# Putting transposed 16-bit planes back together on ScalarE and GpSimd, in place of ScalarE alone

## The chip, the cores and the metric

The kernel runs on one core of a Trainium2 chip. The metric is the device time of one execution in microseconds (us), taken as the median of several runs. The engines are named as in the profile: PE is TensorE, with PEld for its weight loads; DVE is VectorE, ACT is ScalarE, POOL is GpSimd, and SP is the engine that issues nearly all DMAs here (SPq is its queue). Every engine works through its own list of instructions strictly in the order in which that list was written, and waits where a datum or a buffer is not there yet.

## The reference: what is computed

Top-k attention for 4 batches of 8 heads (576 positions, head size 64), whose output is the input of a mixture of 8 experts with Sinkhorn-balanced gates:

```python
scores = q @ k.T / sqrt(64)                     # per batch and head, 576 x 576
kth    = 32nd largest of each row
attn   = softmax(where(scores >= kth, scores, -1e9))
x      = (attn @ v) as 2304 rows of 512
P      = exp(x @ w_gate - max); 8 rounds of normalising rows and columns
out    = sum over 8 experts e of P[:, e] * (relu(x @ w1[e]) @ w2[e])
```

## The kernel before

All of it is one program whose instructions are put in order ahead of time: each part has a priority, and a planner with estimated durations writes one list for each engine. Attention has priority over the expert matmuls, which fill TensorE between its pieces. So while attention runs, TensorE alternates between scores (L122, L123), weighing the values (L281) and expert matmuls (L488, L601).

**Attention.** For two heads at a time and tiles of 128 queries, TensorE makes scores in `sp`, a PSUM tile of which there is one; ScalarE copies them to `s` (L134); VectorE finds the 32 largest in four rounds of MAX8 and MATCH_REPLACE8 (L144, L147); GpSimd makes a bias `eb` (L148); ScalarE runs two passes over the row (L150, L151); GpSimd and VectorE make the reciprocal sum (L199, L200), and GpSimd scales the weights (L203). The weights `Et` (queries on partitions) must then be turned, so that keys are on partitions, into the tile `at` (one buffer), which the matmuls of L281 read.

**The turning.** For the first two stages TensorE turns them. Once more than four pieces of `x` exist, a DMA does, and it turns 16-bit elements. `cross` therefore splits the 32-bit weights on ScalarE into two planes of 16-bit halves (`halves`, L164), has SP issue the transposing DMA into `turned` (L168), and appends to the list `turning` a function `whole` that interleaves the two turned planes into `at` (L171). `land` runs what is in that list. It is called with `tc.issue_after(...)`, which puts the instructions of the block that are on the same engine behind a given one: behind the second pass of a later softmax (`topk`) or behind the next split (`cross`). `halves` and `turned` have one buffer each. A smaller variant, `cross_rest` (L181 to L194), does the same for the 64 left-over queries, and is left as it is.

**Experts.** Weights are loaded into `wr` (3 buffers, L470), rounded to `wh` on ScalarE (L83) and the rest `wl` computed on GpSimd (L86); `wh` and `wl` have 6 buffers each. ScalarE writes the hidden layer `hh` (L556) and VectorE its rest `hl` (L557); ScalarE moves outputs out of PSUM (`y`, L609). After attention, from about 1030 us on, only expert work is left.

Of the kernel before, what the change touches and what calls it, by code (L numbers as in the profile page):

```python
# [9 lines left out]
U16 = mybir.dt.uint16  # L10
AF = mybir.ActivationFunctionType
# [40 lines left out]
def kernel(  # L52
# [11 lines left out]
    nc = tc.nc  # L64
# [93 lines left out]
    def land():  # L158
        while turning:
            turning.pop(0)()  # L160

    def cross(Et, at):
        halves = ap_.tile([128, 2, 2 * S], U16, name="halves", bufs=1)
        split = nc.scalar.activation(halves, Et.bitcast(U16).rearrange("p a (b h) -> p h (a b)", h=2), AF.Copy)  # L164
        with tc.issue_after(split.ins):
            land()
        turned = ap_.tile([128, 2, 9, 128], U16, name="turned", bufs=1)
        nc.sync.dma_start_transpose(turned.rearrange("p h g c -> p (h g) c"), halves.rearrange("p h k -> p (h k)"))  # L168

        def whole():  # L170
            nc.scalar.activation(at.bitcast(U16).rearrange("p g (c h) -> p g c h", h=2),  # L171
                                 turned.rearrange("p h g c -> p g c h"), AF.Copy)

        turning.append(whole)

# [705 lines left out]
```

## Time and profile before

| | |
|---|---|
| median of 3 runs | 1831.21 us (1831.04 to 1831.55) |
| the profiled execution's own time | 1833.39 us |
| its span, first to last instruction | 1831.6 us |
| mean granted TensorE clock | 0.996 of full speed |
| instructions | 26304 |

The rows further down come from the profiled execution. The profiler's span is 1.8 us shorter than that execution's own time, which itself is 2.2 us above the median. A matmul's end in the profile is modelled, so that matmuls overlap on paper: with 512 columns each is shown at about 0.39 us, while the next one starts 0.23 us later. Engine idle times therefore are best read where the next start is late.

### The profile page before, as it was taken

What the parts mean: (1) busy time and instruction counts of PE and PEld (TensorE: products, weight loads), DVE (VectorE), ACT (ScalarE), POOL (GpSimd) and SP (SyncE); (2) the same over time, 40 slices, a digit from 0 to 9 for tenths busy, and PEclk for the clock granted to TensorE, in tenths of its full rate; (3) what the DMA queues carried; (4) which work ended last, traced back from release to release, by engine and by line L of the source; (5) the groups of instructions that cost most, each with busy time, mean ns of one, the idle gap of its engine ahead of it and who ended that gap; (6) DMA issues with size and microseconds to landing.
All of it is one profiled execution on the core that took longest, in us unless ns stands there. A gap on an engine that the chain in (4) does not pass through costs nothing.

```text
span 1831.6 us, 26304 instructions
## 1 busy us (share of the span) xinstructions
PE 1785.6 (97%) x9385; PEld 1480.7 (81%) x9385; DVE 1207.9 (66%) x2232; ACT 1187.6 (65%) x1785; POOL 1068.3 (58%) x842
## 2 busy tenths in 40 slices
PE   4989999999999999999999999999999999999998
PEld 3777888888888878777787889888888888888887
DVE  8999998988888878878787141255555555533333
ACT  5888899999999888988897645533333333333331
POOL 4367856656766585556564688955544554554441
PEclk9999999999999999999999999999999999999999
DMA  4885877765767575656655356423333333211111
GB/s 136 264 260 174 255 198 178 207 191 160 199 174 179 143 223 170 168 152 164 172 152 142 90 174 217 161 98 109 114 117 104 104 107 114 90 58 63 53 35 46
DMA packets 227203, 270.77 MB, mean 148 GB/s; under 512 B 142464, under 2 KB 146688, under 8 KB 227072
## 3 DMA queue, kind: packets, MB, share of 16 engines
q1 hardware_dynamic: 226928, 268.83, 49.8%
q8 instruction: 73, 1.20, 0.3%
q14 instruction: 58, 0.48, 0.1%
q10 hardware_dynamic: 144, 0.26, 0.0%
HBM read 202.19 MB, written 34.60 MB: 129 GB/s over the span
## 4 chain that ended last, share of the span: by engine, by line
PE 83%; ACT 4%; POOL 4%; DVE 3%; DMA 3%; issue 3%; SPq 0%; ACTq 0%; POOLq 0%
PE p L601 20%; PE p L775 19%; PE p L488 18%; PE p L713 10%; PE pc L713 5%; PE pt L281 4%; DMA wr<-in_w_dram 2%; PE pb L713 2%; POOL wl L86 2%; PE sp L122 2%; PE sp L123 2%; DVE m L144 1%; DVE w L147 1%; PE p L524 1%; ACT wh L83 1%
## 5 line engine op out<-in xcount | busy, mean ns | idle before, releaser
L86 POOL TENSOR_TENSOR wl<-wr,wh 128x1024 fp32r<-128x1024 f32 x288 | 694.0, 2422 | 456.2 <-ACT wh L83 445.7
L83 ACT ACTIVATE wh<-wr 128x1024 fp32r<-128x1024 f32 x288 | 304.1, 1061 | 284.4 <-PE p L713 191.2
L144 DVE MAX8 m<-w 128x8 f32<-128x576 f32 x432 | 320.6, 753 | 5.8
L488 PE MATMUL p<-xh,wh 128*128 128x256 f32 (+1 forms) x832 | 274.7, 330 | 2.8 <-DVE hl L557 1.9
L488 PE MATMUL p<-xl,wh 128*128 128x256 f32 (+1 forms) x832 | 273.7, 329 | 0.1
L488 PE MATMUL p<-xh,wl 128*128 128x256 f32 (+1 forms) x832 | 273.0, 328 | 0.0
L601 PE MATMUL p<-wh,hh 128*128 128x512 f32 x640 | 250.2, 396 | 4.3 <-ACT hh L556 2.8
L601 PE MATMUL p<-wl,hh 128*128 128x512 f32 x640 | 249.6, 392 | 0.0
L601 PE MATMUL p<-wh,hl 128*128 128x512 f32 x640 | 241.3, 392 | 0.0
L147 DVE MATCH_REPLACE8 w<-m,w 128x576 f32<-128x576 f32 x288 | 213.7, 743 | 0.0
L775 PE MATMUL p<-wh,h2h 128*128 128x512 f32 x512 | 199.1, 389 | 0.6 <-DVE acc L618 0.6
L775 PE MATMUL p<-wl,h2h 128*128 128x512 f32 x512 | 199.2, 389 | 0.0
L775 PE MATMUL p<-wh,h2l 128*128 128x512 f32 x512 | 196.3, 389 | 0.0
L618 DVE SCALAR_TENSOR_TENSOR acc<-p,P,acc 128x512 f32<-128x512 f32 x120 | 89.5, 750 | 160.4 <-PE p L775 160.4
L557 DVE SCALAR_TENSOR_TENSOR hl<-p,hh 128x512 fp32r<-128x512 f32 x160 | 109.0, 682 | 106.5 <-ACT hh L556 105.5
L488 PEld LDWEIGHTS p<-xh,wh 128*128 128x128 f32 x832 | 157.6, 189 | 20.8 <-issue 2.1
L488 PEld LDWEIGHTS p<-xl,wh 128*128 128x128 f32 x832 | 157.7, 189 | 15.7 <-issue 0.9
L488 PEld LDWEIGHTS p<-xh,wl 128*128 128x128 f32 x832 | 157.6, 189 | 14.2 <-issue 0.5
L144 DVE MAX8 m<-s 128x8 f32<-128x576 f32 x144 | 108.4, 753 | 85.3 <-ACT s L134 84.8
L601 PEld LDWEIGHTS p<-wh,hh 128*128 128x128 f32 x640 | 120.1, 188 | 31.7 <-ACT hh L556 5.3
L601 PEld LDWEIGHTS p<-wl,hh 128*128 128x128 f32 x640 | 120.6, 188 | 23.4 <-issue 0.4
L601 PEld LDWEIGHTS p<-wh,hl 128*128 128x128 f32 x640 | 119.9, 188 | 23.6 <-DVE hl L557 0.2
(171 smaller groups left out, 3550.4 us busy)
## 6 DMA issues: line engine op xcount, KB each, us to landing
wr<-in_w_dram SPq DMA_DIRECT2D x248, 512.0 KB, 3.5
y<-y SPq DMA_DIRECT2D x160, 256.0 KB, 2.8
raw<-in_k_dram SPq DMA_DIRECT2D x48, 288.0 KB, 3.7
p<-y SPq DMA_DIRECT2D x32, 256.0 KB, 4.0
wr<-in_w_dram SPq DMA_DIRECT2D x32, 256.0 KB, 4.3
yp<-p SPq DMA_DIRECT2D x32, 256.0 KB, 3.3
raw<-in_q_dram SPq DMA_DIRECT2D x31, 256.0 KB, 3.5
values<-in_v_dram SPq DMA_DIRECT2D x24, 256.0 KB, 3.6
```

Of the source, the lines that this page charges most:

```text
L83: nc.scalar.activation(dst, src, AF.Copy)
L86: nc.gpsimd.tensor_tensor(dst, src, hi.bitcast(F32), op=OP.subtract)
L122: nc.tensor.matmul(o, qc, kh[:, cs], start=(i == 0), stop=False)
L144: nc.vector.max(m8[:, u, r, :], ws[u] if r else units[u][0])
L147: nc.vector.match_replace(ws[u], m8[:, u, r, :], ws[u] if r else units[u][0], LOWEST)
L281: weighed = nc.tensor.matmul(av[r, 0:n], vr[:, o:o + 64], at[:, block, 0:n], start=(j == order[0]), stop=(j == order[-1]))
L488: nc.tensor.matmul(ps[:, fo, :], a[:, kk, fs], x[:, k0 + kk, cs], start=(i == 0), stop=(i == 3 * nk - 1))
L557: nc.vector.scalar_tensor_tensor(seat.hl[:, ft, cs], src, 0.0, seat.hh[:, ft, cs].bitcast(F32), op0=OP.max, op1=OP.subtract)
L601: nc.tensor.matmul(ps, a[:, ft, ts], m[:, ft % 2, :], start=(i == 0), stop=(i == 3 * NFT - 1))
L618: return nc.vector.scalar_tensor_tensor(ACC[t], y, g, ACC[t], op0=OP.mult, op1=OP.add)
L713: nc.tensor.matmul(ps, w[:, kk, :], x[:, kk, :], start=(fresh and i == 0), stop=(i == 5), skip_group_check=True)
L775: nc.tensor.matmul(ps, a[:, ft, ts], m[:, ft, :], start=(i == 0), stop=(i == 11))
```

## The change

The one ScalarE instruction of `whole`, which writes all 2304 16-bit elements of each partition, becomes two: ScalarE writes the elements with index 0 of each pair, and GpSimd those with index 1. Each half reads one plane in order and writes every other 16-bit element of `at`. The smaller variant in `cross_rest` stays on ScalarE.

```diff
         def whole():
-            nc.scalar.activation(at.bitcast(U16).rearrange("p g (c h) -> p g c h", h=2),
-                                 turned.rearrange("p h g c -> p g c h"), AF.Copy)
+            au = at.bitcast(U16).rearrange("p g (c h) -> p g c h", h=2)
+            two = turned.rearrange("p h g c -> p g c h")
+            nc.scalar.activation(au[:, :, :, 0], two[:, :, :, 0], AF.Copy)
+            nc.gpsimd.tensor_copy(au[:, :, :, 1], two[:, :, :, 1])
 
         turning.append(whole)
```

## Rows read from the trace of the kernel before

**Rows 1.** The page, parts 1 and 2: busy time; tenths in 40 slices.
```profile
PE 1785.6 (97%) x9385; PEld 1480.7 (81%) x9385; DVE 1207.9 (66%) x2232; ACT 1187.6 (65%) x1785; POOL 1068.3 (58%) x842
...
PE   4989999999999999999999999999999999999998
```

**Rows 2.** Windows: length, busy us (count) of PE, PEld, DVE, ACT, POOL; clock; DMA.
```profile
220.00:1030.00 810.00, 804.19 (x4612) 664.92 (x4610) 658.60 (x1291) 728.69 (x1056) 488.36 (x428) 1.00 0.64 174
...
1110.00:1800.00 690.00, 689.53 (x3160) 575.98 (x3159) 309.66 (x428) 248.44 (x352) 372.97 (x243) 1.00 0.31 99
```

**Rows 3.** Waits of PE, 220 to 1030 us: us in total, times, longest.
```profile
PE sp L122 <- ACT s L134: 1.8, 2, 1.4
PE p L601 <- ACT hh L556: 1.6, 1, 1.6
PE p L601 <- ACT y L609: 1.4, 1, 1.4
PE p L488 <- DVE hl L557: 0.8, 2, 0.6
```

**Rows 4.** Tile `turned`: duration ns min/median/max; waiters (us, times); landings.
```profile
L168 SPq DMA_TRANSPOSE turned<-halves x48: 2405/2740/4628, 222.6 to 1009.8; - x48
L171 ACT ACTIVATE at<-turned x48: 2381/2404/2447, 233.0 to 1016.6; 128x2304 uint16<-128x2304 uint16 x48
...
  PEld pt L281: 0.4, 1
...
DMA to landing us min/median/max: 3.3/4.6/7.1
```

**Rows 5.** Groups by form, ACT, 220 to 1030 us: busy us, mean ns.
```profile
L164 ACT ACTIVATE halves<-Et 128x2304 uint16<-128x2304 uint16 x48 | 101.9, 2124 | 15.3 <-POOL Et L203 13.9 <-DMA turned<-halves 1.1
...
L181 ACT ACTIVATE halves<-Et 128x1152 uint16<-128x1152 uint16 x12 | 14.0, 1169 | 6.1 <-DMA turned<-halves 3.8 <-POOL Et L203 2.2
```

**Rows 6.** Groups by form, POOL, 220 to 1030 us.
```profile
L86 POOL TENSOR_TENSOR wl<-wr,wh 128x1024 fp32r<-128x1024 f32 x128 | 306.9, 2410 | 120.9 <-ACT wh L83 112.5 <-PE p L488 4.6 <-issue 2.5
L203 POOL TENSOR_SCALAR Et<-Et,st 128x576 f32<-128x576 f32 x107 | 79.0, 750 | 25.6 <-DVE st L200 23.8 <-PE sp L123 0.7 <-PE p L488 0.3
...
L86 POOL TENSOR_TENSOR qm<-raw,qm 64x256 fp32r<-64x256 f32 x15 | 11.1, 738 | 1.2 <-POOL eb L148 0.2
...
L199 POOL TENSOR_SCALAR st<-st 128x2 f32<-128x2 f32 x47 | 9.0, 191 | 51.4 <-ACT Et L151 49.4
```

**Rows 7.** Timeline of PE around three gaps: start us, us, [idle before].
```profile
419.58 0.50 PE L601 MATMUL p<-wh,hh 128*128 128x512 f32 x1 [1.62 <-ACT hh L556]
...
817.16 0.50 PE L601 MATMUL p<-wh,hh 128*128 128x512 f32 x1 [1.41 <-ACT y L609]
...
842.04 0.40 PE L122 MATMUL sp<-kh,qs 128*128 128x288 f32 x1 [1.38 <-ACT s L134]
```

**Rows 8.** Timeline of ACT, the same three places.
```profile
416.66 2.39 ACT L171 ACTIVATE at<-turned 128x2304 uint16<-128x2304 uint16 x1
418.95 0.57 ACT L556 ACTIVATE hh<-p 128x512 fp32r<-128x512 f32 x1
...
811.51 2.40 ACT L171 ACTIVATE at<-turned 128x2304 uint16<-128x2304 uint16 x1
813.82 0.63 ACT L134 ACTIVATE s<-sp 128x576 f32<-128x576 f32 x1
814.35 0.77 ACT L150 ACTIVATE Et<-s,m 128x576 f32<-128x576 f32 x1
...
839.08 2.39 ACT L171 ACTIVATE at<-turned 128x2304 uint16<-128x2304 uint16 x1
841.37 0.62 ACT L134 ACTIVATE s<-sp 128x576 f32<-128x576 f32 x1
```

**Rows 9.** Timeline of DVE, second place: start us, us.
```profile
812.79 0.76 DVE L144 MAX8 m<-w 128x8 f32<-128x576 f32 x1
```

**Rows 10.** Waits of PEld, and of SP's queue, 220 to 1030 us.
```profile
PEld p L601 <- POOL wl L86: 0.3, 1, 0.3
...
SPq L470 <- POOL wl L86: 163.3, 67, 5.5
```

## The prediction

> **What bounds the kernel now.** I read the busy times first, because they say which engine can set the end at all. TensorE is busy for 97% of the span and every other engine for 66% or less, and after the first slices its row of tenths shows nothing but nines [rows 1]. So the time is the sum of TensorE's work, which this change leaves alone, and of the gaps in it. A change on two other engines can only move gaps.
>
> Next, the windows, to see which gaps lie where the change acts. All 48 instructions that it replaces start between 233.0 and 1016.6 us [rows 4]. In the stretch from 220 to 1030 us TensorE is busy for 804.19 of 810 us, at full clock: 5.8 us of gaps. In the expert stretch after it, from 1110 to 1800 us, the gaps are 0.5 us [rows 2]. The start of the kernel has many more, but lies ahead of the first changed instruction. This gives the size of the question: if every gap of the stretch vanished, the kernel would gain 5.8 us, 0.3%. The loss has no such cap.
>
> Then the waits of TensorE in that stretch. They sum to 5.6 us, and 4.8 of them name ScalarE: the score copy 1.8, the hidden layer 1.6, the output copy 1.4; the other 0.8 names VectorE [rows 3]. GpSimd is not among them, and weight loads waited for its `wl` for 0.3 us once [rows 10]. In the same stretch ScalarE is busy for 728.69 us (90%) and GpSimd for 488.36 (60%) [rows 2]. The engine that loses work is the one that TensorE waits for; the one that gets it is not.
>
> Last, the timeline at the three large gaps, to see what held ScalarE there. Each has a whole copy L171 ahead of the late instruction. At 416.66 the copy runs 2.39 us, the hidden layer `hh` starts behind it at 418.95, and TensorE, after a gap of 1.62, goes on at 419.58. At 839.08 it runs 2.39 us, the score copy follows at 841.37, and TensorE goes on at 842.04 after 1.38. At 811.51 it runs 2.40 us, and behind it stand a score copy at 813.82, the softmax passes from 814.35 on and the output copy for which TensorE waited 1.41 us until 817.16 [rows 7, 8]. These three are 4.4 of the 5.8 us.
>
> **The ScalarE half.** Removed: 48 instructions of 2.404 us on 2304 elements [rows 4]. Added: 48 on 1152 elements, reading in order and writing every other 16-bit element. The nearest row has the same count and a stride on the other side: L181, 1.169 us [rows 5]. Below, the bound is half of L164, 2.124 / 2 = 1.062, which pretends that the fixed cost halves as well; above it is half of L171 plus a fixed cost taken from L164 and L181, 2 x 1.169 - 2.124 = 0.214, half of which is missing when an instruction is cut in two: 2.404 / 2 + 0.107 = 1.309 [rows 4, 5]. I take 1.169. ScalarE saves 48 x 1.235 = 59 us (53 to 64), and its share of the stretch falls from 90% to 83%.
>
> In the three gaps, if the order holds, what follows the copy starts 1.235 us sooner. At the first and third nothing else is in the way: 1.235 each. At the second the first softmax pass also needs the MAX8 that runs from 812.79 for 0.76 us, to 813.55 [rows 9], so it can start 0.80 us before its 814.35, and I count 0.80. Sum: 3.3 us (3.0 with the dear half, 3.5 with the cheap one).
>
> **The GpSimd half.** GpSimd has no copy of 16-bit elements in this trace. The nearest row is its one-input instruction, L203: 0.750 us for 576 elements; with L199 (0.191 us for 2) that is 0.974 ns an element and a fixed 0.19, so 0.19 + 1152 x 0.974 ns = 1.31 us. The upper bound is the pace of the two-input L86: (2410 - 738) / (1024 - 256) = 2.18 ns an element, so 0.19 + 2.51 = 2.70 us [rows 6]. The lower bound is half the one-input pace, should narrow elements go two at a time: 0.75 us. I take 1.31, since the copy has one input. That adds 48 x 1.31 = 63 us (36 to 130), and GpSimd's share of the stretch goes from 60% to 68% (65% to 76%): busy, not full.
>
> By these rows the dear end is where two operands are read, which the copy does not do. The Trainium skill, GPSIMD Engine Reference, section "Engine selection", says the same with a warning: elementwise work does not belong on GpSimd, about 2x slower than VectorE with two inputs, while one input is roughly line rate. Its section on cycle accounting has 2.6 cycles an element at 1.2 GHz, which as an estimate would make this copy some 2.5 us; at that price `at` would be whole no earlier than now. No run here shows it yet for 16-bit elements.
>
> **What the copy stands among on GpSimd.** Behind it in GpSimd's list come `eb`, the reciprocal sum's L199, the scaling L203 and the `wl` rounding. Cover: GpSimd is idle for 322 of the 810 us, 120.9 of it ahead of `wl`, nearly all waiting for ScalarE's `wh` [rows 2, 6]; that wait shortens as ScalarE is relieved. SP's weight loads do stand for `wl` to free their buffer, 163.3 us in all [rows 10], without TensorE ever going short. So I cost it at nothing in the sum, and at what follows under the rivals if the cover fails.
>
> **Waits that the change adds.** `at` is whole when the later of two engines is done, and `turned` is free for the next transposing DMA likewise. TensorE waited for L171 0.4 us in one place [rows 4], so there is little to win or lose there. On ScalarE the half copy still stands behind a softmax pass or a split; the GpSimd half has no such order of its own and may be written into GpSimd's list right behind the expected landing.
>
> **Sum.** Gaps shortened: -3.3. Since all the lists are written anew with other durations, gaps will not stay where they are; I give back a third of the gain, 1.1, for one of the three opening again elsewhere. That is -2.2 us. On the profiled execution: 1833.4 - 2.2 = 1831.2; on the median of the runs, 2.2 lower: 1831.2 - 2.2 = 1829.0 us. About 0.2%, 3.7 us, is what a measurement of this kernel can tell from no change, so this counts as no change.
>
> **The rivals.**
>
> *ScalarE's relief closes nearly all gaps.* With 7% of its time freed, the score copies, hidden layers and outputs that TensorE waits for come sooner everywhere, not just behind L171. For it: 4.8 of 5.6 us of the waits name ScalarE. Against: gaps must shrink by two thirds to be seen. Between -3.7 and the whole 5.8: about -4.7, 1826.5 us.
>
> *GpSimd holds up the softmax.* The copy stands at the head of GpSimd's list until the transposed planes land, 3.3 to 7.1 us after issue, median 4.6 [rows 4], so up to 2.5 us later than the usual. `eb` or L203 behind it are late, then ScalarE's softmax pass, which is in its list ahead of a score copy or hidden layer that TensorE needs; there is only one `sp`. Priced: if a third of the 48 copies pass on 0.7 us each, +11; less the 3.3 gained, +8: 1839 us. It decides once the copies pass on more than 3.3 + 3.7 = 7.0 us in all, 0.15 us each. For it: ScalarE is in order and 83% full, so a late pass moves what is behind it; a copy at 2.70 us would do the same without any late landing. Against: GpSimd's 322 idle us, and hardly a wait of TensorE that names it.
>
> *Nothing happens.* The gaps move and keep their sum: 1831 us. This differs from my forecast by less than can be measured, so I put it into the same case.
>
> **How the numbers follow.** The forecast with its neighbour, from 1827.6 to 1834.9: 0.43. ScalarE's relief closing more: 0.28, which is the chance of faster. GpSimd holding things up: 0.29, the chance of slower. The cap on gains is 5.8 us by busy times, so the low end is 1825.0. Above, I leave out the far tail of the slower case and end at 1838.5. The forecast's own range is 1827.6 to 1831.5.
>
> **What would show each step.** L171 on ScalarE at 1.06 to 1.31 us and 48 of them; a GpSimd copy at 0.75 to 2.70 us; ScalarE's busy time down by 53 to 64 us and GpSimd's up by 36 to 130. TensorE's gaps between 220 and 1030 us at about 3.6 instead of 5.8, with no wait of 1.4 us or more behind L171. The expert stretch unchanged. The prediction is wrong if TensorE's waits there grow beyond some 9 us, and the mechanism of the slower rival is confirmed if GpSimd's copy is then seen waiting for DMA with `eb` or L203 late behind it.

## The result and the profile after

The change makes the kernel slower. Four runs give a median of 1844.6 us (1840.5 to 1847.4) beside 1831.2 us before on the same chip: a ratio of 1.0072, 95% interval 1.0057 to 1.0087, or 13.4 us. The forecast was 1829.0 us in a range of 1825.0 to 1838.5. The profiled execution took 1844.79 us, with a span of 1842.7 us (1831.6 before).

In the kernel after, code lines behind the edit move by two: TensorE's expert matmuls are L490 and L603 (L488 and L601 before), the hidden layer and its rest L558 and L559, the weight load L472. ScalarE's half is L173, GpSimd's is L174.

The busy times, part 1 of the page, answer to [rows 1]:

```profile
PE 1788.0 (97%) x9385; PEld 1481.1 (80%) x9385; DVE 1206.9 (65%) x2232; ACT 1145.7 (62%) x1785; POOL 1138.3 (62%) x890
```

The change did what it says. ScalarE lost 41.9 us, GpSimd gained 70.0, and TensorE has the same 9385 instructions. The windows (columns as in [rows 2]) show in which stretch the time went:

```profile
220.00:1030.00 810.00, 798.93 (x4540) 660.64 (x4539) 656.21 (x1292) 684.13 (x1051) 555.91 (x475) 1.00 0.65 173
...
1110.00:1800.00 690.00, 688.19 (x3165) 575.60 (x3164) 307.00 (x425) 251.79 (x355) 377.88 (x246) 1.00 0.32 102
```

TensorE's gaps in the changed stretch grew from 5.8 to 11.1 us, at the same full clock, and only 4540 matmuls start in it (4612 before). ScalarE, which was to be relieved, is relieved (728.69 to 684.13), and still TensorE is worse supplied. The expert stretch has 1.8 us of gaps where it had 0.5. The span grew by 11.1 us in all: the rest is mainly 2 us more of gaps ahead of 220 us, where the lists are still the same, and 2.4 us more of modelled busy time for the same matmuls.

The price of the two halves is in the rows of the tile `turned`, beside [rows 4]:

```profile
L168 SPq DMA_TRANSPOSE turned<-halves x48: 2403/2890/4613, 222.9 to 1001.9; - x48
L174 POOL COPY at<-turned x48: 1484/1510/1713, 229.5 to 1010.2; 128x1152 uint16<-128x1152 uint16 x48
L173 ACT ACTIVATE at<-turned x48: 1489/1512/1554, 243.2 to 1020.3; 128x1152 uint16<-128x1152 uint16 x48
...
  DMA turned<-halves: 27.8, 14
  PE pt L283: 7.7, 4
```

Each half takes 1.51 us, so ScalarE saves 0.89 us per copy where 1.235 had been counted. The last two lines are GpSimd standing idle at the head of its list: 27.8 us in 14 places until the planes have landed, and 7.7 us in 4 places until TensorE has read the previous `at`. The first is what the slower rival had named, and one would stop here. But the waits of TensorE in the stretch, beside [rows 3], do not name GpSimd:

```profile
PE p L490 <- DVE hl L559: 8.1, 5, 2.6
PE p L603 <- ACT hh L558: 1.1, 3, 0.6
PE pt L283 <- ACT at L173: 0.7, 1, 0.7
PE p L490 <- DVE st L202: 0.6, 1, 0.6
PE sp L122 <- ACT s L134: 0.4, 1, 0.4
```

They sum to 10.9 us, and 8.1 of them are five waits for VectorE's `hl`, which was 0.8 before. The largest of them, in the timeline of the engines (start, duration, and in brackets the idle time ahead):

```profile
338.04 1.17 ACT L183 ACTIVATE halves<-Et 128x1152 uint16<-128x1152 uint16 x1
...
338.18 0.76 DVE L144 MAX8 m<-s 128x8 f32<-128x576 f32 x1 [0.45 <-ACT s L134]
...
338.86 0.74 DVE L144 MAX8 m<-w 128x8 f32<-128x576 f32 x1
...
339.09 0.31 ACT L184 ACTIVATE halves<-Et 128x128 uint16<-128x128 uint16 x1
...
339.29 1.49 ACT L173 ACTIVATE at<-turned 128x1152 uint16<-128x1152 uint16 x1
...
339.45 0.29 PE L123 MATMUL sp<-kl,qs 128*128 128x288 f32 x1
...
339.58 0.74 DVE L147 MATCH_REPLACE8 w<-m,s 128x576 f32<-128x576 f32 x1
...
340.24 0.15 DVE L202 RECIPROCAL st<-st 128x2 f32<-128x2 f32 x1
340.31 0.68 DVE L554 TENSOR_TENSOR p<-p,yp 128x512 f32<-128x512 f32 x1
...
340.63 0.58 ACT L558 ACTIVATE hh<-p 128x512 fp32r<-128x512 f32 x1
340.90 0.75 DVE L144 MAX8 m<-w 128x8 f32<-128x576 f32 x1
...
341.56 0.67 DVE L559 SCALAR_TENSOR_TENSOR hl<-p,hh 128x512 fp32r<-128x512 f32 x1
...
342.38 0.55 PE L490 MATMUL p<-xh,wh 128*128 128x256 f32 x1 [2.64 <-DVE hl L559]
```

Read it upwards. TensorE waits for a PSUM tile `p` that `hl` still reads. `hl` needs `hh`, and `hh` stands on ScalarE behind three copies of the turning, 2.6 us in one go (L183, L184 and the half L173). But `hh` is done at 341.21, and `hl` does not start before 341.56: from 338.18 on VectorE works, without idle time, through what stands ahead of `hl` in its own list, steps of the search for the 32 largest above all. The other four waits for `hl` look the same: VectorE is busy right up to `hl`, and `hh` had been done 0.6 to 3.0 us earlier. So what ends last there is what VectorE's list puts ahead of `hl`, and VectorE is an engine whose instructions the change does not touch.

So there are two suspects: the new instructions (their work and their waits), and the lists. The lists of before and after are the same up to the first GpSimd copy at 229.5 us. From there on the planner has put all five engines' instructions in another order.

### The profile page after: what moved, and what is told of

The parts are those of the page before. It is cut to its first block, busy times and chain, and to the rows that moved or that the text cites. A ratio compares the mean times of both kernels' runs of the same rounds, so it can differ in the third digit from the quotient of the medians.

```text
span 1842.7 us, 26405 instructions
## 1 busy us (share of the span) xinstructions
PE 1788.0 (97%) x9385; PEld 1481.1 (80%) x9385; DVE 1206.9 (65%) x2232; ACT 1145.7 (62%) x1785; POOL 1138.3 (62%) x890
## 4 chain that ended last, share of the span: by engine, by line
PE 69%; ACT 9%; DVE 7%; DMA 6%; POOL 4%; issue 4%; SPq 0%; ACTq 0%; POOLq 0%
PE p L777 19%; PE p L490 14%; PE p L603 13%; PE p L715 9%; PE pc L715 5%; DVE m L144 3%; DMA wr<-in_w_dram 3%; PE pt L283 3%; DVE w L147 2%; POOL wl L86 2%; PE pb L715 2%; ACT wh L83 2%; PE sp L122 1%; PE sp L123 1%; ACT Et L151 1%
## 5 line engine op out<-in xcount | busy, mean ns | idle before, releaser
L490 PE MATMUL p<-xh,wh 128*128 128x256 f32 (+1 forms) x832 | 276.6, 332 | 10.9 <-DVE hl L559 9.1
L490 PE MATMUL p<-xl,wh 128*128 128x256 f32 (+1 forms) x832 | 274.5, 330 | 0.0
L490 PE MATMUL p<-xh,wl 128*128 128x256 f32 (+1 forms) x832 | 274.0, 330 | 0.3 <-POOL wl L86 0.3
L603 PE MATMUL p<-wh,hh 128*128 128x512 f32 x640 | 249.4, 396 | 4.1 <-ACT hh L558 3.9
L603 PE MATMUL p<-wl,hh 128*128 128x512 f32 x640 | 250.2, 393 | 0.0
L603 PE MATMUL p<-wh,hl 128*128 128x512 f32 x640 | 242.3, 392 | 0.0
L559 DVE SCALAR_TENSOR_TENSOR hl<-p,hh 128x512 fp32r<-128x512 f32 x160 | 108.9, 682 | 149.0 <-ACT hh L558 147.6
L490 PEld LDWEIGHTS p<-xh,wh 128*128 128x128 f32 x832 | 158.9, 191 | 31.4 <-DVE hl L559 9.9
L490 PEld LDWEIGHTS p<-xl,wh 128*128 128x128 f32 x832 | 159.0, 191 | 15.4 <-issue 0.5
L490 PEld LDWEIGHTS p<-xh,wl 128*128 128x128 f32 x832 | 158.7, 191 | 15.2 <-POOL wl L86 0.8
L603 PEld LDWEIGHTS p<-wh,hh 128*128 128x128 f32 x640 | 119.8, 188 | 30.0 <-ACT hh L558 5.5
L603 PEld LDWEIGHTS p<-wh,hl 128*128 128x128 f32 x640 | 120.1, 188 | 24.0 <-issue 0.4
L603 PEld LDWEIGHTS p<-wl,hh 128*128 128x128 f32 x640 | 120.5, 188 | 22.7 <-POOL st L201 0.4
```

Of the source, the lines that this page charges most:

```text
L490: nc.tensor.matmul(ps[:, fo, :], a[:, kk, fs], x[:, k0 + kk, cs], start=(i == 0), stop=(i == 3 * nk - 1))
L559: nc.vector.scalar_tensor_tensor(seat.hl[:, ft, cs], src, 0.0, seat.hh[:, ft, cs].bitcast(F32), op0=OP.max, op1=OP.subtract)
L603: nc.tensor.matmul(ps, a[:, ft, ts], m[:, ft % 2, :], start=(i == 0), stop=(i == 3 * NFT - 1))
```

## The experiments

To tell the two apart, most kernels below plan once, keep the five lists, and then run other instructions in them. "Old lists" are those of the kernel before, "new lists" those of the changed kernel; the 48 copies of `whole` are all that differs from them, and every other instruction keeps its place.

```python
_, _, plan = build(PLAN, None)      # plans, and returns the order
for k in plan:                      # second build: ties each instruction to the one ahead of it
    i = shared[k]
    if i.engine in last:
        tc.add_manual_dep(i, last[i.engine].name, info, reason="order of another plan")
    last[i.engine] = i
```

Where GpSimd's copy is added to old lists, it stands where ScalarE's stands in the order over all engines, if nothing else is said. Times are medians in us. "Gaps" are 810 us less TensorE's busy time in the windows row from 220 to 1030 us of the profiled execution. The kernel before took 1830.7 (x), 1831.9 (y), 1832.0 (z), 1831.8 (w) and 1831.1 us (v) on the chips of the five groups, so a difference between runs of two groups can be off by about 1 us; where it matters, each run is taken against the kernel before on its own chip.

| run | lists | ScalarE | GpSimd | us | ratio to before (95%) | gaps |
|---|---|---|---|---|---|---|
| before | old | whole | nothing | 1831.2 | | 5.8 |
| after | new | half | half | 1844.6 | 1.0057 to 1.0087 | 11.1 |
| x1 | old | half | half | 1837.4 | 1.0025 to 1.0053 | 8.8 |
| x2 | new | whole | nothing | 1874.8 | 1.0224 to 1.0252 | 26.7 |
| x3 | own, copy later | half | half | 1854.8 | 1.0117 to 1.0144 | 19.4 |
| x4 | own | two halves | nothing | 1849.2 | 1.0089 to 1.0117 | 14.4 |
| y1 | old | half | nothing | 1824.8 | 0.9950 to 0.9975 | 1.5 |
| y2 | old | whole | reads 9 elements | 1837.4 | 1.0020 to 1.0046 | 9.4 |
| y3 | old | whole | reads 1152 elements | 1848.0 | 1.0072 to 1.0100 | 13.6 |
| y4 | old | whole | as much work, no wait | 1835.4 | 1.0013 to 1.0030 | 7.7 |
| z1 | new | half | nothing | 1839.9 | 1.0026 to 1.0053 | 10.4 |
| z2 | new | half | reads 9 elements | 1840.9 | 1.0033 to 1.0062 | 10.7 |
| z3 | old | half | half, placed | 1833.4 | 1.0002 to 1.0019 | 6.8 |
| z4 | old | half | nothing (VectorE: half, placed) | 1835.9 | 1.0010 to 1.0028 | 8.0 |
| w1 | of y2's program | whole | nothing | 1838.6 | 1.0022 to 1.0049 | 8.9 |
| w2 | own | half | nothing | 1846.0 | 1.0066 to 1.0092 | 14.0 |
| w3 | of w2 | half | half | 1857.1 | 1.0125 to 1.0157 | 22.0 |
| w4 | of y2's program | half | half, planner's place | 1885.3 | 1.0285 to 1.0317 | 35.2 |
| v1 | old | half | half, placed again | 1827.4 | 0.9975 to 0.9993 | 2.1 |
| v2 | old | 36 halves, 12 whole | 36 halves, placed | 1826.2 | 0.9960 to 0.9981 | 1.4 |

Eleven of the 18 runs came out outside every range that was expected of them: x1 (by 0.6 us), x2, x3, y1, y3, y4, z1, z3, w2, w4 and v1.

**x1 and x2: lists or instructions?** x1 runs the changed instructions in the old lists, x2 the old instructions in the new lists.

```diff
-    _, _, plan = build(new, None); build(new, plan)     # the changed kernel
+    _, _, plan = build(old, None); build(new, plan)     # x1
+    _, _, plan = build(new, None); build(old, plan)     # x2
```

> The changed instructions, but every engine's list in the order of the kernel before; GpSimd's copy stands where the global order of the old plan has ScalarE's. If the rewritten lists are what costs the 13 us (theory A), this is at or a little below the kernel before: 1828 to 1832 us, with the three gaps behind L171 shorter by some 0.9 us each. If the copy on GpSimd itself costs it, by its length or by waiting for the landing at the head of the list (theory B), it is 1838 us or more.

> The other way round: the one ScalarE instruction of the kernel before, in the lists that the changed kernel has; no copy on GpSimd. Theory A (lists): it stays slow, 1840 to 1850 us, since ScalarE even has 43 us more to do than in the changed kernel. Theory B (GpSimd's copy): back to 1829 to 1834 us.

Neither alone: x1 keeps 6.7 of the 13.4 us, so the split costs something in lists that have nothing else against it. x2 is 44 us slower than before, far beyond both theories: lists that were planned with the half copy serve the whole one badly. How x1 loses its time is seen at its largest gap, in the timeline (there L197 and L198 are the halves, L191 the transposing DMA on SP's queue, L499 the weight load, L106 the rounding `wh`, L630 the second expert matmul):

```profile
656.69 1.51 ACT L197 ACTIVATE at<-turned 128x1152 uint16<-128x1152 uint16 x1
...
660.17 2.41 POOL L109 TENSOR_TENSOR wl<-wr,wh 128x1024 fp32r<-128x1024 f32 x1
...
662.54 1.49 POOL L198 COPY at<-turned 128x1152 uint16<-128x1152 uint16 x1
...
664.06 2.68 SPq L191 DMA_TRANSPOSE turned<-halves  x1
...
666.78 0.58 SPq L499 DMA_DIRECT2D wr<-in_w_dram  x1
...
671.49 1.06 ACT L106 ACTIVATE wh<-wr 128x1024 fp32r<-128x1024 f32 x1 [4.38 <-DMA wr<-in_w_dram]
...
672.60 0.50 PE L630 MATMUL p<-wh,hh 128*128 128x512 f32 x1 [3.07 <-ACT wh L106]
```

The same place in the kernel before:

```profile
656.91 2.39 ACT L171 ACTIVATE at<-turned 128x2304 uint16<-128x2304 uint16 x1
...
659.33 2.67 SPq L168 DMA_TRANSPOSE turned<-halves  x1
...
662.10 0.53 SPq L470 DMA_DIRECT2D wr<-in_w_dram  x1
```

ScalarE's half is done at 658.20. GpSimd comes to its own only behind a weight rounding and ends at 664.03. `turned` has one buffer, so the next transposing DMA stands on SP until 664.06, and the weight load in SP's list behind it until 666.78. Before, the whole copy ended at 659.30, the DMA went at 659.33 and the load at 662.10. The load is now 4.7 us late, ScalarE stands 4.38 us for it and TensorE 3.07. The wait names ScalarE, and yet GpSimd's late copy is at the head of the chain.

**x3 and x4: move the copy, or undo the second engine, and plan anew.** In x3 the copy may not stand in GpSimd's list ahead of the scaling L205 of the softmax at hand; in x4 ScalarE makes both halves.

```diff
-        with tc.issue_after(split.ins):                                          # x3
+        with tc.issue_after(split.ins), tc.issue_after(scaled.ins):
-            nc.gpsimd.tensor_copy(au[:, :, :, 1], two[:, :, :, 1])               # x4
+            nc.scalar.activation(au[:, :, :, 1], two[:, :, :, 1], AF.Copy)
```

> Both halves as changed, but GpSimd's copy is queued behind the scaling of the next tile's weights, as ScalarE's half is behind the next split, so that it no longer stands waiting for the transposed planes; the lists are planned anew. If the head-of-list wait for the landing is the cost (theory B1): 1828 to 1832 us, and no GpSimd wait for DMA. Theory A: the lists differ again from both kernels, so anything from 1828 to 1846 us, not tied to the wait.

> Both halves as instructions of ScalarE, nothing on GpSimd; lists planned anew. ScalarE has 48 x (2 x 1.51 - 2.40) = 30 us more than before. Theory B: no copy on GpSimd, so near the kernel before, at most some 3 us above for the fuller ScalarE: 1831 to 1835 us. Theory A: other lists, other gaps, 1835 to 1850 us.

x3 cut GpSimd's waits for the planes from 27.8 to 8.6 us and is 10 us slower than the changed kernel: a loss of this size does not need those waits. x4 gives ScalarE 0.6 us more per copy than the kernel before, nothing to GpSimd, and loses 18 us. As both were planned anew, neither says more than that.

**y1 to y4: relief, waits and work, each alone in the old lists.**

```diff
             nc.scalar.activation(au[:, :, :, 0], two[:, :, :, 0], AF.Copy)
-            nc.gpsimd.tensor_copy(au[:, :, :, 1], two[:, :, :, 1])               # y1: without it
+            nc.scalar.activation(au, two, AF.Copy)                               # y2, y3, y4: whole, and
+            nc.gpsimd.tensor_copy(spare, two[:, :, 0, 1])                        # y2
+            nc.gpsimd.tensor_copy(spare, two[:, :, c * 64:(c + 1) * 64, 1])      # y3, c = 0 and 1
+            nc.gpsimd.tensor_copy(spare, constant)                               # y4, twice 576 elements
```

The kernels that run ScalarE's half alone (y1, and z1, z2 and w2 below) leave the other half out: it keeps what stood in `at` (the expectations call that zero, but the first two stages write whole weights there). They also hold one tile `at` for the whole program, which GpSimd clears once at the start. ScalarE's copy waited for no `at` before the change, and does not in y1.

> Lists of the kernel before; ScalarE writes its half, and the other half is left out (it stays zero), so GpSimd has nothing more to do. What ScalarE's relief is worth by itself: by the forecast's gaps, with the half at 1.51 us in place of 1.17, 0.89 + 0.80 + 0.89 = 2.6 us below the kernel before, 1828 us; 1831 if the gaps open again elsewhere.

> Lists of the kernel before; ScalarE's whole copy stays, and where the split kernel has GpSimd's copy, GpSimd copies 9 elements of the turned planes into a spare tile (0.1 to 0.2 us). It has the waits of the copy without its work: it stands until the planes land, and the next transposing DMA waits for it. Theory S (these waits, above all SP's list behind the DMA): 1834 to 1838 us. Theory W (GpSimd's work makes everything behind it late): 1831 to 1832 us.

> As the run with the tiny read, but GpSimd copies all 1152 elements into a spare tile, in two instructions of 576. Waits and work, without ScalarE's relief and without the dependence of the weighing on it. Theory S and W both: some 7 to 10 us above the kernel before, 1838 to 1841 us; if it is near 1831, the cost was in the completion of the turned weights, which this leaves alone.

> As the run with the full read, but GpSimd copies from a constant tile: the work at the same places, with no wait for the planes and nothing that waits for it. Theory W: as slow as the full read, 1838 to 1841 us. Theory S: 1831 to 1834 us.

The relief of ScalarE alone is worth 7.1 us. The waits of TensorE in y1 are all but gone (L636 and L523 are the expert matmuls there):

```profile
PE p L636 <- ACT hh L591: 0.7, 1, 0.7
PE p L523 <- DVE hl L592: 0.6, 1, 0.6
PE sp L146 <- ACT s L158: 0.2, 1, 0.2
```

The first and the third row are what is left of two of the three gaps that the prediction named: 0.68 us of 1.62 and 0.24 of 1.38; the one of 1.41 is gone. In x1 they are 0.67, 0.25 and gone as well. So the relief does there what was forecast, 3.5 us beside 3.3, and x1 loses its time elsewhere.

Against it stand 5.5 us for the waits that GpSimd's instruction brings (y2), 3.5 for its work (y4), and 16.1 for both together (y3): more than their sum of 9.0. Why is not shown: y3 keeps GpSimd busy, and it also reads `turned` for 1.1 us longer than y2 each time; no run takes the two apart.

**z1 to z4: the same in the new lists, and the copy where GpSimd is idle.** z1 and z2 take GpSimd's copy out of the new lists, wholly or but for a read of 9 elements. In z3 and z4 the place of each copy is read off the trace of y1: the first at which the engine is free after the planes have landed.

```diff
+AHEAD = [134, 136, 150, 154, ...]          # z3: GpSimd instructions ahead of each of the 48 copies
+        for x in ahead.get(count, []):     # behind the n-th instruction of the engine's old list
+            put(x)
-            nc.gpsimd.tensor_copy(au[:, :, :, 1], two[:, :, :, 1])               # z4, with places of its own
+            nc.vector.tensor_copy(au[:, :, :, 1], two[:, :, :, 1])
```

> The five lists of the changed kernel, GpSimd's 48 copies taken out and nothing else moved; ScalarE makes its half and the other half stays zero, which the output leaves out. With the old lists the same cut took 1824.8 us. If the rewritten lists themselves cost time, this one stays clearly above that: 1830 to 1836. If they cost nothing and the changed kernel's 13 us are GpSimd's copy alone (its wait for the planes and its 1.5 us of work), it comes to 1824 to 1827.

> As z1_new_lists_half, but in each place of GpSimd's list where the changed kernel copies, GpSimd reads 9 elements of the planes (0.2 us) into a spare tile: its waits without its work; the lower half stays zero, which the output leaves out. If GpSimd's standing at the head of its list for the landing (27.8 us in the changed kernel) is the cost, this takes 5 us or more above z1_new_lists_half; if the 1.5 us of work is, it takes less than 2 us above it, and the rest of the way to 1844.6 is work.

> The old lists and both halves as in x1_old_lists_split (1837.4 us), but each GpSimd copy stands where GpSimd, in the run with ScalarE's half alone, first had its hands free after the planes had landed. If the cost of the split in the old lists is the waits (GpSimd standing at the planes, the transposing DMA and the weight load on SP standing behind a late copy), this comes to 1824.8 + 2 to 4 for the work = 1827 to 1830, faster than the kernel before. If GpSimd's 72 us of added work costs what it does wherever it stands, it stays at 1834 to 1838.

> As z3_old_lists_placed, but VectorE copies the lower half, each copy placed by the same rule in VectorE's list. VectorE is 81% busy in this stretch, and its residual is the last step ahead of many matmuls. If an engine's own spare time is what counts, 48 copies of about 1.2 us put into gaps cost 1 to 3 us over 1824.8: 1826 to 1828. If VectorE's residuals are pushed back by them, TensorE waits more for them (0.6 us before) and it takes 1831 to 1838.

z1 shows that the lists lose time by themselves. It has no GpSimd copy, and still the waits of the changed kernel, nearly number by number (L527 and L640 are the expert matmuls):

```profile
PE p L527 <- DVE hl L596: 8.1, 6, 2.6
PE p L640 <- ACT hh L595: 1.1, 2, 0.8
PE p L527 <- DVE st L232: 0.6, 1, 0.6
```

The gap of 2.64 us is there too, one us earlier, with `hl` at 340.59 right behind a MAX8 at 339.92:

```profile
341.41 0.35 PE L527 MATMUL p<-xh,wh 128*128 128x256 f32 x1 [2.64 <-DVE hl L596]
```

z1 and y1 run the same instructions and differ in nothing but their order: 1839.9 beside 1824.8 us, or 15.0 us for the order when each is taken against the kernel before on its own chip. In these lists GpSimd's waits add 1.1 us (z2), no more than the runs scatter, though GpSimd stands for the planes there even longer than in the changed kernel, 40.0 us in 21 places. The whole copy adds 5.5 us (13.4 less z1's 7.9). In the old lists the same copy costs 13.7 (x1 over y1).

z3 falls between its two theories. It is 5.2 us better than x1, by placing alone (each against the kernel before on its chip), but 8.6 us short of y1. One place of z3 shows a mistake in the placing, in the timeline (L207 is GpSimd's copy, L118 the rounding `wl`, L319 the matmuls that read `at`):

```profile
439.80 1.52 POOL L207 COPY at<-turned 128x1152 uint16<-128x1152 uint16 x1 [4.50 <-PE pt L319]
441.23 7.09 POOL L118 TENSOR_TENSOR wl<-wr,wh 128x1024 fp32r<-128x1024 f32 x3
...
446.02 0.50 PE L639 MATMUL p<-wl,hh 128*128 128x512 f32 x1 [2.28 <-POOL wl L118]
```

The planes had landed, but TensorE was still reading the previous `at`, which has one buffer. GpSimd stood there for 4.50 us with three weight roundings behind it, and TensorE lost 2.28. z4 shows that VectorE is no better a helper: its copy takes 1.47 us, and TensorE's waits for `hl` come to 5.4 us.

**w1 to w4: are these new lists bad, or any new lists?** The planner's input is varied and what runs is fixed: the program of y2 gives the lists for w1 and w4, that of y1 the lists for w2 and w3.

```diff
-    _, _, plan = build(old, None)
+    _, _, plan = build(whole_and_tiny_read, None)   # w1 runs old instructions, w4 the changed ones
+    _, _, plan = build(half_alone, None)            # w2 runs the half alone, w3 the changed ones
```

> The same instructions as the kernel before (one whole ScalarE copy), in lists planned for a program that also has GpSimd read 9 elements of the planes in 48 places; those reads are left out of what runs. The lists differ from the old ones from about a third of the way on. If the old lists are a lucky draw, and any planning anew costs 10 us or more, this takes 1838 to 1850. If planning anew costs nothing in itself, it takes 1829 to 1834.

> ScalarE's half alone (the other half stays zero, which the output leaves out) in lists planned for just that. In the old lists it took 1824.8 us, in the changed kernel's lists 1839.9. If the planner misjudges the half copy, or any planning anew costs, this takes 1834 to 1842 too. If only the lists with GpSimd's copy in them are bad, it takes 1822 to 1828.

> The whole change (both halves, 48 GpSimd copies, each put into GpSimd's list where ScalarE's half stood in the plan) in the lists of w2_half_own_lists. In the old lists the copies cost 12.6 us over the half alone, in the changed kernel's lists 4.7. If waits and work of the copy add to whatever the lists give, this takes 5 to 13 us more than w2_half_own_lists; if they are hidden in slack that a worse plan has, less than 5.

> The whole change in the lists of w1_redrawn_lists_whole, the GpSimd copies standing where the planner had put the reads of 9 elements. If the planner's own place for GpSimd's instruction is what the old lists lacked, this is faster than w1_redrawn_lists_whole by the relief of ScalarE less 3 to 5 us, that is 2 to 4 us faster than it; if the waits and the work cost what they cost in the old lists, it takes 5 to 7 us more than it.

w1 runs the very instructions of the kernel before, in lists that leave the old ones late (SP's at about 392 us, GpSimd's at 678), and takes 6.8 us more. w2 has less work than the kernel before, in lists planned for just that work, and takes 14 us more than it and 21 more than the same instructions in the old lists. So the new lists are no special case. Of the sets that were planned afresh, three can be set against the old lists at equal instructions, and all lose: 6.8 (w1), 15.0 (z1) and 21.4 us (w2, the last two beside y1). x3 loses too, 17 us against x1 with the changed instructions, though its copy also stands elsewhere. w3 adds 11 us for the copies to w2.

w4 was expected within some us of w1 and takes 47 us more. The planner's places for the short read often lie ahead of the landing, and a real copy in them is disastrous (waits, all engines, 220 to 1030 us):

```profile
POOL at L202 <- DMA turned<-halves: 95.1, 28, 8.3
...
PE p L528 <- DVE hl L597: 7.9, 4, 3.5
...
PE p L641 <- ACT hh L596: 6.5, 6, 1.7
PE p L641 <- POOL wl L109: 6.3, 5, 3.1
```

GpSimd stands for 95.1 us, late enough for TensorE to wait for `wl` itself. This is the slower rival's mechanism at full strength, which the changed kernel has only in part (27.8 us).

**v1 and v2: a version that beats both.** v1 moves the 11 copies of z3 that were reached before `at` was free or that delayed a weight rounding. v2 leaves 12 copies whole on ScalarE, those for which y1's trace shows GpSimd no gap of about 1.5 us, and splits 36.

```diff
-AHEAD = [..., 215, ..., 247, ..., 274, ..., 319, 331, ..., 351, 360, 376, ..., 404, ..., 435, ..., 542, ...]
+AHEAD = [..., 216, ..., 249, ..., 275, ..., 326, 332, ..., 353, 368, 377, ..., 412, ..., 440, ..., 547, ...]
-            if SPLIT:                                                            # v2
+            if SPLIT and NTH[0] - 1 not in (1, 11, 14, 15, 16, 22, 23, 25, 26, 27, 30, 33):
```

> As z3_old_lists_placed (1833.4 us), with 11 of the 48 GpSimd copies moved further back in GpSimd's list, so that none is reached before the tile that it writes is free, nor ahead of a weight rounding that it would delay. If these places are the rest of the cost (TensorE waited 3.3 us for the roundings there), this takes 1829 to 1831. If GpSimd's added work costs it wherever it stands, it stays at 1833 to 1835.

> As v1_placed_again, but the 12 copies for which GpSimd has no gap of 1.5 us between the landing and the next use stay whole on ScalarE, as before the change; 36 are split, each where GpSimd stood idle. If the copy is free exactly where GpSimd idles, this keeps most of ScalarE's relief (7.1 us for 48) and takes 1825 to 1828, faster than the kernel before. If the relief needs all 48, or the work costs in any place, 1830 to 1834.

v1 takes 1827.4 us, some 5 less than z3 (each against the kernel before on its chip), for 11 places in one engine's list. v2 takes 1826.2 us (1823.8 to 1827.6), ratio 0.9970 with an interval of 0.9960 to 0.9981: 4.9 us faster than before and 18 faster than the changed kernel. The two are not told apart by these runs. TensorE's waits of 220 to 1030 us in v2 are down to two:

```profile
PE p L642 <- ACT hh L597: 0.7, 1, 0.7
PE p L529 <- DVE hl L598: 0.6, 1, 0.6
```

Its windows row of the same stretch, with gaps of 1.35 us:

```profile
220.00:1030.00 810.00, 808.65 (x4678) 671.46 (x4677) 659.89 (x1290) 704.73 (x1073) 549.56 (x473) 1.00 0.64 174
```

And the tile `turned`, with the halves and the copies that stayed whole:

```profile
L209 ACT ACTIVATE at<-turned x36: 1487/1514/1551, 230.4 to 1007.1; 128x1152 uint16<-128x1152 uint16 x36
L210 POOL COPY at<-turned x36: 1486/1513/1545, 230.6 to 1005.8; 128x1152 uint16<-128x1152 uint16 x36
...
L213 ACT ACTIVATE at<-turned x12: 2388/2406/2441, 243.3 to 783.2; 128x2304 uint16<-128x2304 uint16 x12
```

GpSimd does 36 copies, with a busy share of the stretch of 68%, as the prediction had it for all 48, and no wait of TensorE is left that names it.

## Why the prediction was wrong

Two steps of the sum failed. The first is its last term: "Since all the lists are written anew with other durations, gaps will not stay where they are; I give back a third of the gain, 1.1". The sentence names the right cause and gives it a fraction of its size: with ScalarE's half alone, the order costs 15.0 us (z1 against y1), with both halves 6.8 (the changed kernel against x1). The second is GpSimd's copy, "So I cost it at nothing": it costs 5.5 us in the new lists (the changed kernel against z1) and 13.7 in the old ones (x1 against y1).

Each against the kernel before on its own chip, the 13.4 us measured are 7.1 of relief won, 15.0 lost to the lists and 5.5 to the copy; or, in the other order, 7.1 won, 13.7 lost to the copy and 6.8 to the lists. The terms depend on the order in which they are taken, because lists and instructions suit or do not suit each other, so neither can be called the cause of the 13 us alone: from the changed kernel, the old order alone wins back 6.8 us, leaving the copy out alone 5.5, and both together 20.5. Each term carries some 2 to 4 us of doubt, since the runs of the changed kernel and of z1 scatter by 7 us.

Point by point:

- *TensorE sets the end and its gaps are the question*: right in every run of the table, where the time rises with the gaps on the whole.
- *The cap of 5.8 us on gains*: too low. y1 gained 7.1 with 1.5 us of gaps left. Busy time ends with modelled matmul ends, and so hides part of the waiting: the same 9385 matmuls are busy for 1785.6 us before and for 1781.0 in y1, and at 342.38 in the changed kernel the profile shows 2.64 us idle, but the next matmul was due 0.13 us (the pace of the ones before) after 339.45, and is 2.80 us late.
- *The ScalarE half*: 1.169 us taken, 1.309 as upper bound, 1.51 measured. L181 has the stride where it reads, this copy where it writes. The relief per copy was 0.89 instead of 1.235.
- *What the relief is worth*: the three gaps named shrank by 3.5 us in the old lists, 3.3 had been counted, although the half was dearer than forecast, which is in part luck. The whole relief is 7.1 us in y1 (for 48 x 0.89 = 43 us of ScalarE's time). The rival of closing nearly all gaps, priced at 4.7, was the better reading, and y1 went beyond it.
- *The GpSimd half*: 1.31 us taken, 1.51 measured, far from the dear end of 2.70. The estimate of some 2.5 us came from a figure that does not fit this copy: in the Trainium skill, GPSIMD Engine Reference, section "Elementwise — side-by-side cycle accounting", the 2.6 cycles an element are those of `tensor_tensor` with two inputs. The copy has one, and its trace has 1.51 us.
- *"So I cost it at nothing"*: wrong. In the old lists, as much work without a wait costs 3.5 us (y4) and the waits without the work 5.5 (y2). The cover was there (60% busy), but not at the places where the lists had put the copy; with 36 copies in the gaps of y1's trace (v2), most of the relief remains.
- *Waits that the change adds*: "there is little to win or lose there" looked only at TensorE's wait for `at`. It named that `turned` comes free when the later engine is done, and did not follow it into SP's list, where a weight load stands behind the transposing DMA. x1's largest gap, 3.07 us, is that chain.
- *GpSimd holds up the softmax*: right in sign, and its sign of recognition, GpSimd waiting for the DMA, is there with 27.8 us. Its price, 1839 us, even lay above the end of the stated range. But take the copy away and 7.9 us of loss stay (z1), and 40.0 us of such waits without the work cost 1.1 (z2). It is not what makes the new lists slow; only w4, with 95.1 us, shows it at full strength.

What stays open is why the old lists are better than the others from the same planner. The runs show that they are, and at single gaps which instruction stands ahead of which: four of the five `hl` that TensorE waits for have 2 to 10 more MAX8 ahead of them in VectorE's new list than in the old one. They do not show a property that sets the good lists apart, and whether the planner misjudges a particular duration was not tried by itself.

## What to carry to other kernels

Where a planner writes the lists, a two-line edit is two changes: the instructions, and a new order for everything behind them. Freeze the old lists and run the new instructions in them before judging either; here the order alone was worth 6.8 to 15.0 us, as much as what the edit itself gave or took. Work that is moved to an idle engine is free only at the places where the trace shows that engine idle after its inputs have landed and its output buffer is free, and the waits to look for lie behind it: in the queue that waits for the buffer it frees, and in what stands in that queue.

## What the runs showed of the hardware

- Cutting the interleaving copy in two costs more than the copy: 1510 and 1494 ns for the two halves on ScalarE (x4) beside 2404 ns for both in one instruction [rows 4]. Per element written that is 1.30 ns against 1.04.
- The same 1152 16-bit elements, read in order and written to every other place, take about as long on three engines: 1.51 us on ScalarE and GpSimd, 1.47 on VectorE (z4). GpSimd's copy of 576 elements took 0.667 us (y3), of 9 elements 0.20 us (y2).
- Runs of one kernel on one chip can lie 7 us apart: so do the four of the changed kernel, while the four of the kernel before on that chip lie within 0.5 us, and its 23 on the chip of the z runs lie 7.4 us apart.
